# Reordering the first twenty-four products of batch 0, and loading and using the last four 128-row blocks of w_out in two slices

## The chip, the cores and the metric

The kernel runs on one core of one Trainium2 chip. Its time is the device time of one execution in microseconds (us). Most executions of one kernel agree within about 0.1% here. The span of a profile is the time from its first to its last instruction; it is 1.7 to 1.9 us shorter than the device time of the same run.

Names of engines: PE is TensorE's matmul unit, PEld its weight load, DVE is VectorE, ACT is ScalarE, POOL is GpSimd, SP is SyncE. PSUM and SBUF are two memories of the core: in this kernel the matmuls write their sums to PSUM and read what they multiply from SBUF. "L465" means line 465 of the kernel file. Lines below the change have other numbers in other files (the last products are L912 in before and L917 in after).

## The reference, cut to what matters

```python
def _attn_ref(q, k, v, g_norm):            # q, k, v: 8 batches, 8 heads, 576 rows, 64
    kv = np.einsum('bhsd,bhse->bhde', k, v)
    out = np.einsum('bhsd,bhde->bhse', q, kv)
    rms = np.sqrt(np.mean(out * out, axis=-1, keepdims=True) + 1e-06)
    return (out / rms * g_norm).astype(np.float32)

def _moe_ref(x, w_in, w_out):              # x: 4608 x 512, w_in: 512 x 2048, w_out: 2048 x 512
    h = x @ w_in
    g = np.where(h > 0.0, h, np.exp(np.minimum(h, 0.0)) - 1.0)
    return (g @ w_out).astype(np.float32)
```

(The factor alpha of the reference, 1.0, is left out.) The attention output of all heads is the x of the second part. The kernel takes 512 of the 576 rows of one batch as a group, and the 64 left over of every batch as a ninth; batch 0 is special, because everything is still being loaded when it starts.

## The kernel before

Two matrix products per group take nearly all of PE's time. The first, x times w_in, is made as 16 column blocks f of 128, each the sum of 4 chunks c of 128 rows, so 64 matmuls of 128x512. After each pair of blocks, ACT and DVE apply the ELU (`elu`), which frees the pair's PSUM. The second, g times w_out, adds 16 terms f for each of four row groups j.

In batch 0 the first six blocks are made by a special piece of code, because chunk c of x exists only when its normalisation is done:

```python
pair = ps_head.tile([P, 2, G], FP32, name="h_ps", tag="kv")
products = {0: pair[:, 0, :], 1: pair[:, 1, :], 2: bank(6), 3: bank(7), 4: bank(0)}
first((0, 1, 2, 3), (0,))        # blocks, chunks: one matmul for each combination, chunk by chunk
mean_first(3); log_first(3); exp_first(3); scale_first(3)    # makes chunk 3 of x, on PE, ACT, DVE
products[5] = bank(1)
first((0, 1, 2, 3), (1, 2))
first((4, 5), (0, 1, 2))
first((0, 1, 2, 3, 4, 5), (3,))
...
for i, parts in enumerate([[(0, 2, pair)]] + single):
    elu(0, i, parts, i == 1)()
head.close()                      # PSUM of the start is given back ...
ps_at = ...; ps_m1 = ...; ps_m2 = ...    # ... and divided anew into the pools of the main loop
for i in range(3, 8):             # blocks 6 to 15, in pairs; i = 3 is the fourth pair
    mm1(0, i, relu=i in (3, 5, 7), home={5: "m2", 6: "at"}.get(i, "m1"))()
```

`elu` of a pair is an Exp on ACT, then two operations on DVE; the second one reads the products from PSUM again (for the pairs with `relu`, the second and some others, ACT reads them a second time instead). Cut to the case of the first pair:

```python
nc.scalar.activation(e[:, lo:hi, :], ps, AF.Exp)
...
nc.vector.tensor_scalar(out=e[...], in0=e[...], scalar1=1.0, scalar2=1.0, op0=ALU.min, op1=ALU.subtract)
nc.vector.tensor_tensor(out=gT[T][...], in0=e[...], in1=h, op=ALU.max)
```

The loads of w_out go through one queue that POOL issues. "Rows 12 to 14" is short for the blocks 12 and 13 of its 16 blocks of 128 rows, one for each term f. The second product of batch 0 uses them in slices (`hold` puts off the copy of a finished result), with pieces of batch 1's attention put between them:

```python
load_w_out(10, 12)
load_w_out(12, FC)               # FC is 16
fetch_packed_q(2)                # q, then k and v, of batch 2
...
at["mulu1"]()                    # DVE writes the second half of xs of batch 1
unpack_q(2, Q)
ahead["qd"]()
for j in range(J):               # J is 4
    mm2(0, j, 12, FC, hold=j > 1)
    if j == 2:
        at["xu1"](scores[:, 1, :])
mm2_out(0, 2)
mm2_out(0, 3)
...
for i in range(8):               # first product of batch 1
    mm1(1, i, ...)
```

`xu1`, the "turn" in what follows, transposes the second half of batch 1's xs with 8 PE transposes into PSUM, and one DVE operation (L422) copies the result, scaled, to SBUF as chunks 2 and 3 of batch 1's x. The first block of batch 1 needs chunk 2 in its third matmul.

## Time and profile before

| | before |
|---|---|
| median (range of the first 3 runs) | 285.01 us (284.91 to 285.03) |
| span of the profiled run | 283.3 us |
| PE busy | 277.0 us, 98% |
| distance from start to start of two 512-column matmuls | 216 ns |
| only PE wait on the wait list after the first 8 us | 0.3 us, on DVE |

The first and second parts of the page of before say what bounds the kernel:

```profile
PE 277.0 (98%) x2146; PEld 129.2 (46%) x2146; DVE 159.6 (56%) x231; ACT 153.4 (54%) x221; POOL 54.3 (19%) x95
...
PEclk9999999999999999999999999999999999999999
```

PE is busy nearly always, and its granted clock is 90% of full or more in each of the 40 slices (0.998 in the mean). With matmuls at this pace and no less work, only fewer or shorter pauses of PE can make the kernel faster. Pauses must be read with care, for the Trainium skill (Perfetto Trace Analysis, "Tensor Engine Instruction (MATMUL, LD_WEIGHTS)") says that the end of a matmul in a trace is estimated and not observed. This trace agrees: after the head, nearly every 512-column matmul of the full array is shown as 379 ns long (376 to 390), but the next one starts 216 ns after it. So a pause is measured here from start to start, less 216 ns.

The wait list of before (PE only; columns: who waited for whom, total us, times, longest):

```profile
PE bank L596 <- DVE zeros L573: 1.2, 1, 1.2
PE bank L614 <- DVE q_two L150: 0.7, 1, 0.7
PE h_ps L465 <- DVE gT L496: 0.3, 1, 0.3
```

The first two are at the very start. The third is the fifth pair of blocks in batch 0. The chain of waits of before, in order of time, shows what it is made of (start us, duration us, what):

```profile
18.90 0.45 PE h_ps L674 x2
19.35 0.02 issue
19.37 1.03 ACT elu_e L477
20.41 0.02 issue
20.43 0.44 DVE elu_e L488
20.87 0.03 issue
20.89 0.02 DVEq L496
20.91 0.04 issue
20.96 1.23 DVE gT L496
22.19 0.04 issue
22.23 3.61 PE h_ps L465 x16
```

The pair of blocks 0 and 1 is finished by PE at 19.35, read by ACT, and freed by DVE at 22.19. Then the fifth pair, whose PSUM it is, may start. The timeline of PE in before shows the same place (start, duration, engine, line, operation, shapes, count, idle before):

```profile
20.04 1.89 PE L465 MATMUL h_ps<-xT,w_in_sb 128*128 128x512 bf16 x8
22.23 3.61 PE L465 MATMUL h_ps<-xT,w_in_sb 128*128 128x512 bf16 x16 [0.31 <-DVE gT L496]
```

In start times, the last matmul of the fourth pair starts at 21.547 and the first of the fifth at 22.235: 688 ns, so 472 ns lost. The profile's 0.31 us is smaller because the modelled 379 ns still counts as busy.

The turn in the timeline of PE in before:

```profile
45.62 0.61 PE L413 MATMUL se_ps<-ident,xs 128*128 128x128 bf16 x8
46.06 1.03 PE L512 MATMUL o_ps<-w_out_sb,gT 128*128 128x512 bf16 x4
46.92 1.89 PE L465 MATMUL at<-xT,w_in_sb 128*128 128x512 bf16 x8
```

and in the timeline of DVE in before, with the copy that uses them:

```profile
46.34 0.75 DVE L422 TENSOR_SCALAR xT<-se_ps,g_col 128x1024 bf16<-128x1024 bf16 x1 [1.24 <-PE se_ps L413]
```

The copy ends at 47.09. The third matmul of batch 1's first product, the first to read what it wrote, starts at 47.357. It did not have to wait: four matmuls of w_out and two of its own block stood between, and the eight of its line are evenly spaced.

### The profile page before, as it was taken

The page shows a single profiled execution, that of the slowest core. Times are in us where ns is not written, and L with a number is a line of the kernel's source. Part 1 is how long each engine was busy: PE and PEld are TensorE (multiplying, and loading weights), DVE is VectorE, ACT ScalarE, POOL GpSimd, SP SyncE. Part 2 cuts the span into 40 slices and gives each one's busy share as a digit, 9 for nine tenths or more (in the row PEclk, how much of TensorE's full clock was granted, in tenths as well). Part 3 has the DMA queues.
Part 4 walks back from the last instruction along what each step waited for, and adds up shares of the span by engine and source line. Part 5 has one row for each costly group of instructions (what it writes and reads, how often), then busy time and mean ns, then how long its engine had stood idle before and what let it go on. Part 6 is the DMA issues. An engine that isn't in the chain of part 4 may idle for free.

```text
span 283.3 us, 5185 instructions
## 1 busy us (share of the span) xinstructions
PE 277.0 (98%) x2146; PEld 129.2 (46%) x2146; DVE 159.6 (56%) x231; ACT 153.4 (54%) x221; POOL 54.3 (19%) x95
## 2 busy tenths in 40 slices
PE   7999999999999999999999999999999999999994
PEld 2444454445444444444444444444444444444443
DVE  2349543877478646933694468545864586444400
ACT  2769646666486438534773378236923692333311
POOL 7834402161421231005110421012000000000000
PEclk9999999999999999999999999999999999999999
DMA  7999999697994595358934794455233123010122
GB/s 192 203 204 202 206 203 185 218 146 135 194 178 66 152 178 137 74 148 108 212 74 135 104 208 79 117 120 152 50 96 78 78 50 98 0 76 0 74 74 76
DMA packets 56507, 35.99 MB, mean 127 GB/s; under 512 B 32804, under 2 KB 54052, under 8 KB 56484
## 3 DMA queue, kind: packets, MB, share of 16 engines
q0 software_dynamic: 20736, 17.30, 40.1%
q1 hardware_dynamic: 35348, 17.83, 23.8%
q10 hardware_dynamic: 400, 0.52, 0.5%
q8 instruction: 17, 0.28, 0.4%
q14 instruction: 6, 0.05, 0.1%
HBM read 36.70 MB, written 9.44 MB: 163 GB/s over the span
## 4 chain that ended last, share of the span: by engine, by line
PE 95%; DMA 2%; DVE 1%; ACT 0%; issue 0%; SPq 0%; DVEq 0%
PE h_ps L465 41%; PE o_ps L512 39%; PE o_ps L912 5%; DMA st_q<-in_q_dram 2%; PE at L174 2%; PE at L465 1%; PE at L201 1%; PE bank L674 1%; PE h_ps L674 1%; PE bank L596 1%; PE bank L644 1%; PE se_ps L201 1%; DVE gT L496 0%; PE kv_ps L174 0%; ACT elu_e L477 0%; PE at L185 0%
## 5 line engine op out<-in xcount | busy, mean ns | idle before, releaser
L465 PE MATMUL h_ps<-xT,w_in_sb 128*128 128x512 bf16 x536 | 125.8, 379 | 0.3 <-DVE gT L496 0.3
L512 PE MATMUL o_ps<-w_out_sb,gT 128*128 128x512 bf16 x512 | 120.5, 379 | 0.0
L477 ACT ACTIVATE elu_e<-h_ps 128x1024 bf16<-128x1024 f32 (+1 forms) x71 | 70.0, 995 | 81.8 <-PE h_ps L465 79.6
L465 PEld LDWEIGHTS <-w_in_sb 128*128 128x128 bf16 x552 | 52.5, 98 | 64.1 <-DVE xT L333 1.7
L512 PEld LDWEIGHTS <-gT 128*128 128x128 bf16 x512 | 49.4, 98 | 58.4
L488 DVE TENSOR_SCALAR elu_e<-elu_e 128x1024 bf16<-128x1024 bf16 (+1 forms) x75 | 32.2, 429 | 72.5 <-ACT elu_e L477 72.5
L496 DVE TENSOR_TENSOR gT<-elu_e,h_ps 128x1024 bf16<-128x1024 bf16 (+1 forms) x52 | 61.4, 1180 | 5.8 <-DVE elu_e L488 0.5
L525 ACT COPY o_sb<-o_ps 128x512 f32<-128x512 f32 x32 | 18.5, 586 | 15.8 <-PE o_ps L512 15.8
L218 DVE TENSOR_REDUCE ss<-sq 128x16 f32<-128x1024 bf16 x16 | 19.4, 1219 | 10.9 <-ACT sq L213 10.2
L150 POOL COPY q_bf<-q_pk 128x512 bf16<-128x512 bf16 x24 | 14.6, 640 | 22.8 <-DMA q_pk<-in_q_dram 22.8
L483 ACT ACTIVATE elu_h<-h_ps 128x1024 bf16<-128x1024 f32 (+1 forms) x19 | 18.5, 988 | 0.0
L496 DVE TENSOR_TENSOR gT<-elu_e,elu_h 128x1024 bf16<-128x1024 bf16 x19 | 13.2, 692 | 2.8 <-ACT elu_h L483 1.5
L912 PE MATMUL o_ps<-w_out_sb,gT 128*128 128x512 bf16 (+1 forms) x80 | 14.1, 337 | 0.0
L125 POOL COPY gate<-qT 1x1 bf16<-1x1 bf16 x6 | 1.1, 182 | 62.9 <-DMA qT<-q_bf 62.9
L104 POOL DMA_DIRECT2D q_pk<-in_q_dram x14 | 10.5, 755 | 4.0 <-DMA w_out_sb<-in_moe_w_out_dram 1.8
L229 DVE TENSOR_TENSOR xs<-at,ss 128x512 bf16<-128x512 f32 x16 | 10.2, 682 | 1.2 <-ACT ss L225 1.2
L912 PEld LDWEIGHTS <-gT 128*128 128x128 bf16 x80 | 7.7, 98 | 6.4 <-DVE gT L496 0.4
L213 ACT ACTIVATE sq<-at 128x1024 bf16<-128x1024 f32 x9 | 9.4, 1043 | 1.6 <-PE at L201 1.0
L118 POOL DMA_DIRECT2D k_pk<-in_k_dram x12 | 8.3, 692 | 4.6 <-DMA w_in_sb<-in_moe_w_in_dram 2.9
L118 POOL DMA_DIRECT2D v_pk<-in_v_dram x12 | 8.4, 700 | 3.7 <-DMA w_out_sb<-in_moe_w_out_dram 2.1
L596 PE MATMUL bank<-zeros 128*128 128x512 bf16 x20 | 7.4, 495 | 1.2 <-DVE zeros L573 1.2
L920 ACT COPY o_last<-o_ps 128x512 f32<-128x512 f32 (+1 forms) x5 | 2.5, 501 | 10.8 <-PE o_ps L912 10.8
(79 smaller groups left out, 138.2 us busy)
## 6 DMA issues: line engine op xcount, KB each, us to landing
out_dram<-o_sb SPq DMA_DIRECT2D x16, 512.0 KB, 3.0
q_pk<-in_q_dram POOLq DMA_DIRECT2D x14, 256.0 KB, 4.8
k_pk<-in_k_dram POOLq DMA_DIRECT2D x6, 576.0 KB, 8.2
v_pk<-in_v_dram POOLq DMA_DIRECT2D x6, 576.0 KB, 11.5
w_out_sb<-in_moe_w_out_dram POOLq DMA_DIRECT2D x3, 512.0 KB, 14.8
st_q<-in_q_dram SPq DMA_DIRECT2D x2, 512.0 KB, 4.9
w_in_sb<-in_moe_w_in_dram POOLq DMA_DIRECT2D x2, 512.0 KB, 8.9
st_q<-in_q_dram SPq DMA_DIRECT2D x16, 64.0 KB, 2.7
```

The lines of the kernel that those rows point to most:

```text
L104: nc.gpsimd.dma_start(out=t[:, 4 * s : 4 * s + 4].rearrange("p h j d -> p h (j d)"), in_=in_[:, s])
L118: nc.gpsimd.dma_start(out=raw[name, b].rearrange("p h j d -> p h (j d)")[:, hs], in_=in_[:, hs])
L150: eng.tensor_copy(out=out_, in_=in_)
L218: nc.vector.reduce_sum(out=ss, in_=sq.rearrange("p c (h e) -> p (c h) e", h=H), axis=AX.X)
L465: nc.tensor.matmul(h_ps[a][:, cs], lhsT=w_in_sb[:, c, f * P : f * P + P], rhs=x(c, cs), start=(c == 0), stop=(c == KC - 1),)
L477: nc.scalar.activation(e[:, lo:hi, :], ps, AF.Exp)
L483: nc.scalar.activation(h[:, lo:hi, :], ps, AF.Relu)
L488: nc.vector.tensor_scalar(out=e[:, lo:hi, :], in0=e[:, lo:hi, :], scalar1=1.0, scalar2=1.0, op0=ALU.min, op1=ALU.subtract,)
L496: nc.vector.tensor_tensor(out=gT[T][:, 2 * i + lo : 2 * i + hi, :], in0=e[:, lo:hi, :], in1=h, op=ALU.add if relu else ALU.max,)
L512: nc.tensor.matmul(o_ps[T, j], lhsT=gT[T][:, f, j * P : j * P + P], rhs=w_out_sb[:, f, :], start=(f == 0), stop=(f == FC - 1),)
L525: nc.scalar.copy(o_sb[T][:, j % 2, :], o_ps.pop((T, j)))
L912: nc.tensor.matmul(ps, lhsT=gT[B][:, f, j * P : j * P + P], rhs=w_out_sb[:, f, cols], start=(f == 0), stop=(f == FC - 1),)
```

## The change

The intent, as the code suggests: finish blocks 0 to 3 as soon as chunk 3 of x exists, so that ACT and DVE can start on them while PE makes block 5; and because PE is then earlier, let it start on rows 12 and 13 of w_out before rows 14 and 15 have landed.

```diff
     first((0, 1, 2, 3), (1, 2))
-    first((4, 5), (0, 1, 2))
-    first((0, 1, 2, 3, 4, 5), (3,))
+    first((4,), (0, 1, 2))
+    first((0, 1, 2, 3), (3,))
+    first((5,), (0, 1, 2))
+    first((4, 5), (3,))
...
     load_w_out(10, 12)
-    load_w_out(12, FC)
+    load_w_out(12, 14)
+    load_w_out(14, FC)
...
     for j in range(J):
-        mm2(0, j, 12, FC, hold=j > 1)
+        mm2(0, j, 12, 14)
+    for j in range(J):
+        mm2(0, j, 14, FC, hold=j > 1)
         if j == 2:
             at["xu1"](scores[:, 1, :])
```

No matmul and no byte is added or removed. One DMA becomes two.

## The prediction

> **What bounds the kernel.** TensorE. The page gives PE 277.0 of a 283.3 us span (98%), full granted clock in all 40 slices, and a chain of waits that is 95% PE. In the ordered trace a 512-column matmul follows the last every 216 ns, the isolated gap of the Trainium skill (TensorE: Matmul & The Clock Gate, "Back-to-back issue gap"; its sustained 131 ns is not seen here). Matmul ends are estimates, so I reckon start to start. A change can only win where that exceeds 216 ns. The change touches one such place: from 21.547 to 22.235 us, 688 ns, so 472 ns lost (the wait view counts 0.3 us of it, PE h_ps <- DVE gT). The fifth pair of products needs the PSUM pair of the first two: last c=3 matmul of that pair starts 18.957 -> ACT Exp 19.37 to 20.39 -> DVE 0.43 + 1.22 us, done 22.18 -> PE 22.235.
>
> **Part 1, the reorder.** No matmul is added. x0 chunk 3 is written by DVE until 17.965, usable about 18.02 (chunk 2 showed 53 ns from DVE end to PE start); in the new order f=0, c=3 issues at 18.094, so no new stall. The pair is complete three matmuls (647 ns) earlier; Exp starts about 18.73, DVE releases the pair about 21.54, before PE asks at 21.763. The whole 0.47 us goes. The loads have slack enough for PE to stay early: v_pk of batch 1 landed 38.13, used 39.08; w_out rows 10-12 landed 39.38, used 40.80.
>
> **Part 2, split load and slices.** Rows 12-16 landed at 41.94; PE will ask at 42.55 instead of 43.03, so even the unsplit load would just make it. The split costs one more issue on POOL (0.74 us, idle engine), no bytes; rows 12-14 land near 40.7. It buys slack, not time. Later loads on that queue move by under 1 us, off the path.
>
> **What it gives back.** The slices move the transposes of batch 1's second half (xu1). Before, four w_out matmuls plus two of mm1 (c=0, 1) stood between them and the first use of their result; after, only two plus two. Before: first transpose 45.615, DVE copy 46.335 to 47.086, semaphore 47.10, first use 47.357 without wait. From first transpose to usable is 1.52 us; the new order covers 8 transposes (0.447) + 4 x 0.216 = 1.31 us. A new stall of 0.21 us at c=2 of batch 1's first product. The same pattern at 71.540 to 71.902 (362 ns, waiting on DVE xT) shows that such a stall is real.
>
> **Sum.** -0.47 + 0.21 = -0.26 us; after 50 us everything is only shifted: **284.75 us**, range 284.45 to 285.05. Chances: faster by over 2%: 0; within 2%: 0.99; slower: 0.01.
>
> **What would show it.** Right: 216 ns instead of 688 at the fifth pair; first Exp about 18.73; PE never waiting on w_out; about 430 ns start to start before the third matmul of batch 1's first product, released by DVE xT; span about 283.05. Wrong: a stall at f=0, c=3 on x0; a stall on a load between 35 and 45 us; no gap at xu1 (then about 284.55); a growing wait at 70 to 92 us, where DVE waits of 0.15 and 0.19 us exist.
>
> **What would make it wrong.** The load queue pushed back by the extra issue; the copies of the first two outputs, now later on ACT, delaying a PSUM release; run-to-run spread (0.12 us), half the effect.

## The result, and the profile after

| | before | after |
|---|---|---|
| median of 6 runs | 284.98 us (284.83 to 285.06) | 284.75 us (284.56 to 285.67) |
| span of the profiled run | 283.3 us | 283.0 us |
| PE lost before the fifth pair of batch 0 | 472 ns | 0 |
| PE lost at the third matmul of batch 1 | 0 | 214 ns |

The ratio of after to before is 0.9997 (95% interval 0.9984 to 1.001). Ratios and intervals follow the means of the runs more than the medians that are quoted. One of the six runs of after took 285.67 us and pulls that mean up. By the clock alone the change is therefore within noise; the traces have to say whether a gain is there.

The wait list of after, PE only, has lost its third line:

```profile
PE bank L596 <- DVE zeros L573: 1.2, 1, 1.2
PE bank L614 <- DVE q_two L150: 0.5, 1, 0.5
```

The chain of waits of after runs through PE where it had gone through ACT and DVE, and goes through DVE at a place where it had not:

```profile
17.12 1.08 PE bank L674 x5
18.20 0.43 PE h_ps L674 x2
18.64 1.51 PE bank L674 x7
20.15 5.18 PE h_ps L465 x24
...
45.69 0.46 PE se_ps L413 x8
46.15 0.03 issue
46.18 0.02 DVEq L422
46.20 0.05 issue
46.24 0.76 DVE xT L422
47.01 0.04 issue
47.05 1.46 PE at L465 x6
```

The pair is finished ("18.20 0.43 ... h_ps L674 x2", ending 18.64) 0.7 us earlier than in before, and PE goes from the fourth into the fifth pair without a step through another engine. In the timeline of PE in after the two pairs are now one line, and the turn looks like this:

```profile
19.98 4.26 PE L465 MATMUL h_ps<-xT,w_in_sb 128*128 128x512 bf16 x19
...
45.52 0.61 PE L413 MATMUL se_ps<-ident,xs 128*128 128x128 bf16 x8
45.97 0.59 PE L512 MATMUL o_ps<-w_out_sb,gT 128*128 128x512 bf16 x2
46.40 2.10 PE L465 MATMUL at<-xT,w_in_sb 128*128 128x512 bf16 x8
```

Eight matmuls now take 2.10 us, where they took 1.89 in before. That 0.21 us is the whole trace of the new wait on this view. No idle time is printed: the matmul before it starts at 46.619 and is modelled to end at 46.998, so only 51 ns appear idle before the late one starts at 47.049. Start to start it is 430 ns. The wait list leaves it out altogether, but the chain of waits finds it.

The loads, as issue and landing of each part of w_out on the queue (us, read from the trace):

```
rows      before: issued  landed  first used     after: issued  landed  first used
10 to 12          27.20   39.38   40.80                 27.44   39.31   40.28
12 to 14          28.53   41.94   43.03                 28.77   40.59   42.50
14 to 16          with the line above                   31.35   41.92   44.23
```

PE never waited for w_out in either kernel. The four loads behind w_out (q, k and v of batch 2) were issued 1.5 to 2.1 us later in after (the first at 32.78 instead of 31.12, the last at 37.30 instead of 35.22) but landed within 0.1 us of their times in before (43.25 against 43.30, 50.29 against 50.28).

One more reading is needed for the comparisons below. The start of the kernel, up to about 14.5 us, hangs on the first loads and varies between executions: in the eleven traces, the first product of x and w_in starts between 14.24 and 14.62 us. To leave that out, I measure PE's stretch: from the start of the matmul of block 3, chunk 2 (the last one before the orders part) to the start of the kernel's last matmul. It is 261.950 us in before and 261.683 in after: 0.267 us less, against the 0.26 us predicted. It is read from one execution of each kernel; three experiments below that should agree (part1_only, load_split_only, turns_earlier) do so within 0.01 us.

### The profile page after: what moved, and what is told of

It reads as the page before. It is cut to its first block, busy times and chain, and to the rows that moved or that the text cites. A ratio compares the mean times of both kernels' runs of the same rounds, so it can differ in the third digit from the quotient of the medians.

```text
span 283.0 us, 5186 instructions
## 1 busy us (share of the span) xinstructions
PE 277.2 (98%) x2146; PEld 129.4 (46%) x2146; DVE 159.7 (56%) x231; ACT 153.5 (54%) x221; POOL 54.4 (19%) x96
## 4 chain that ended last, share of the span: by engine, by line
PE 95%; DMA 2%; DVE 1%; issue 0%; SPq 0%; ACT 0%; DVEq 0%
PE h_ps L465 42%; PE o_ps L512 39%; PE o_ps L917 5%; DMA st_q<-in_q_dram 2%; PE at L174 2%; PE bank L674 1%; PE at L465 1%; PE at L201 1%; PE h_ps L674 1%; PE bank L596 1%; PE bank L644 1%; PE se_ps L201 1%; PE kv_ps L174 0%; PE at L185 0%; PE se_ps L413 0%; DVE xT L422 0%
```

## The experiments

The theory: PE's time is its matmuls plus the pauses where it waits. The reorder removes one of 0.47 us; the use of w_out in slices creates one of 0.21 us because the turn then has too few matmuls behind it; the split load does neither. The rivals: the split load is needed for the reorder's gain; the extra DMA is what costs 0.2 us; the order of the products counts only by "earlier is better". The first four runs were on one chip, the next four on another, the last on a third, each with runs of before beside it. All gave correct results.

| run | median us (runs) | before beside it (9 or 7 runs) | PE's stretch less that of before | lost before the fifth pair | lost at the turn |
|---|---|---|---|---|---|
| after | 284.75 (6) | 284.98 (6 runs) | -0.27 us | 0 | 214 ns |
| part1_only | 284.50 (5) | 284.92 | -0.48 | 0 | 0 |
| part2_only | 285.21 (5) | 284.92 | +0.20 | 471 ns | 214 ns |
| load_split_only | 284.60 (5) | 284.92 | -0.47 | 0 | 0 |
| turns_earlier | 284.53 (5) | 284.92 | -0.48 | 0 | 0 |
| one_earlier | 284.68 (4) | 285.01 | -0.23 | 256 ns | 0 |
| too_early | 285.13 (4) | 285.01 | +0.09 | 0, but 576 ns at chunk 3 | 0 |
| both_turns | 284.44 (5) | 285.01 | -0.64 | 0 | 0 |
| late_split | 285.53 (4) | 285.01 | +0.57 | 0, but 822 ns on w_out | 215 ns |
| late_whole | 286.60 (4) | 284.94 | +1.52 | 0, but 2005 ns on w_out | 0 |

A caution for who reads such traces: in eight of the nine experiments 31 of the 2146 matmul records are missing (their pages say PE x2115 beside PEld x2146). A missing record looks like a distance of 431 or 432 ns, nearly the same as the real wait at the turn. Where I say that a matmul waited at the turn, all eight matmuls of that block are in the trace and DVE's L422 is what released it.

### part1_only: the reorder without the split

```diff
-    first((4, 5), (0, 1, 2))
-    first((0, 1, 2, 3, 4, 5), (3,))
+    first((4,), (0, 1, 2))
+    first((0, 1, 2, 3), (3,))
+    first((5,), (0, 1, 2))
+    first((4, 5), (3,))
```

> The reorder alone; load and slices as before. Theory: the 688 ns distance in front of the fifth pair becomes 216 ns, rows 12-16 land at 41.9 before PE asks at 42.5, no wait at the third matmul of batch 1's first product: 0.47 us under before, 284.5 us, 0.2 us under the full change. Rival (the split load is what lets PE stay early): a PE wait on w_out near 42.5 us that gives 0.2 us or more back, so 284.75 us or slower.

Measured: 284.50 us, ratio 0.9985 (0.9972 to 0.9997), and PE's stretch 0.48 us shorter than in before. Rows 12 to 16, in one load, landed at 41.59, and PE first used them at 42.25. In the timeline of PE in part1_only the two pairs run on without idle time, and the block after the turn takes 1.89 us:

```profile
19.73 3.62 PE L465 MATMUL h_ps<-xT,w_in_sb 128*128 128x512 bf16 x16
...
46.15 1.89 PE L465 MATMUL at<-xT,w_in_sb 128*128 128x512 bf16 x8
```

So the first part alone is better than the whole change by 0.21 us of PE's stretch, and the rival that the split is needed falls.

### part2_only: the split without the reorder

```diff
-    load_w_out(12, FC)
+    load_w_out(12, 14)
+    load_w_out(14, FC)
...
-        mm2(0, j, 12, FC, hold=j > 1)
+        mm2(0, j, 12, 14)
+    for j in range(J):
+        mm2(0, j, 14, FC, hold=j > 1)
```

> Split load and slices alone; products in the old order. Theory: the fifth pair still waits (688 ns), and a wait of 0.21 us (430 ns start to start) appears at the third matmul of batch 1's first product: 0.21 us over before, 285.2 us. Rival (the split helps by itself): 285.0 or less.

Measured: 285.21 us, ratio 1.0008 (0.9995 to 1.002), PE's stretch 0.20 us longer. Both pauses are there, in the timeline of PE in part2_only:

```profile
22.05 1.24 PE L465 MATMUL h_ps<-xT,w_in_sb 128*128 128x512 bf16 x5 [0.31 <-DVE gT L496]
...
46.31 0.59 PE L512 MATMUL o_ps<-w_out_sb,gT 128*128 128x512 bf16 x2
46.74 2.10 PE L465 MATMUL at<-xT,w_in_sb 128*128 128x512 bf16 x8
```

The two parts add up: -0.48 + 0.20 = -0.28 us, against -0.27 us for both.

### load_split_only: two loads, one slice

```diff
(the reorder, as in part1_only)
-    load_w_out(12, FC)
+    load_w_out(12, 14)
+    load_w_out(14, FC)
```

> The reorder and the split load, but rows 12-16 used in one slice as before. Theory: the new wait comes from the place of the transposes, so it is gone: 216 ns there, 284.5 us as with the reorder alone. Rival (the extra DMA issue causes the loss): the 0.2 us stays, 284.75 us.

Measured: 284.60 us, PE's stretch within 0.01 us of part1_only's, 215 or 216 ns everywhere in the block after the turn, which the timeline of PE in load_split_only shows as

```profile
46.35 1.89 PE L465 MATMUL at<-xT,w_in_sb 128*128 128x512 bf16 x8
```

The extra DMA costs PE nothing; the loss belongs to the use in slices.

### turns_earlier: the whole change, with the turn two matmuls earlier

```diff
         mm2(0, j, 14, FC, hold=j > 1)
-        if j == 2:
+        if j == 1:
             at["xu1"](scores[:, 1, :])
```

> The full change, with the transposes of batch 1's second half one row group earlier (after j=1 instead of j=2 in the last slice, two matmuls earlier). Theory: cover in front of the first use goes from 1.31 to 1.74 us against the 1.52 us needed, the 430 ns distance becomes 216 ns: 284.5 us. xs is ready 0.4 us before. Rival (extra issue): 430 ns stays somewhere, 284.75 us.

Measured: 284.53 us, PE's stretch again that of part1_only (0.003 us apart), and four matmuls of w_out stand behind the turn again. In the timeline of PE in turns_earlier:

```profile
46.40 1.89 PE L465 MATMUL at<-xT,w_in_sb 128*128 128x512 bf16 x8
```

The first transpose to the third matmul of the block is 1.741 us without a wait; in after it is 1.524 us with one. So what the turn needs is 1.524 us, and it is only its place that was wrong.

### one_earlier and too_early: how much earlier is right

one_earlier lets block 5 have two of its three matmuls first, so that the pair is finished one matmul earlier than in before and not three:

```diff
-    first((4, 5), (0, 1, 2))
-    first((0, 1, 2, 3, 4, 5), (3,))
+    first((4,), (0, 1, 2))
+    first((5,), (0, 1))
+    first((0, 1, 2, 3), (3,))
+    first((5,), (2,))
+    first((4, 5), (3,))
```

> A dose: products in an order where the first four finish one matmul (216 ns) earlier than before, instead of three; load and slices as before. Theory: the distance in front of the fifth pair falls by just that, from 688 to about 472 ns; 284.75 us. Rival (any reorder that takes product 5 out of the way frees the whole gap, or the gap depends on ACT and DVE alone): 216 or 688 ns.

Measured: 284.68 us. The distance before the fifth pair is 472 ns, so 256 ns are lost: 216 less than in before, for one matmul of 216 ns. The chain of waits of one_earlier still goes through DVE:

```profile
20.65 1.23 DVE gT L496
21.88 0.04 issue
21.93 1.24 PE h_ps L465 x5
```

too_early puts nothing between chunks 2 and 3:

```diff
-    first((4, 5), (0, 1, 2))
-    first((0, 1, 2, 3, 4, 5), (3,))
+    first((0, 1, 2, 3), (3,))
+    first((4, 5), (0, 1, 2, 3))
```

> The first four products finished with no other product between chunks 2 and 3, then 4 and 5; load and slices as before. Theory: f=0, c=3 would issue at 17.45 but chunk 3 of x0 is usable at 18.02, so PE loses 0.57 us there (788 ns start to start); the fifth pair's gap is gone (216 ns); net +0.10 us, about 285.1 us. Rival (earlier is always better): under 284.6 us.

Measured: 285.13 us, PE's stretch 0.09 us longer than in before. The gap before the fifth pair is gone, and a longer one has opened, where chunk 3 of x is not there yet. In the timeline of PE in too_early:

```profile
17.89 0.59 PE L674 MATMUL h_ps<-xT,w_in_sb 128*128 128x512 bf16 x2 [0.41 <-DVE xT L665]
```

That is 792 ns after the matmul before it, so 576 ns lost. Earlier is not always better: there is a window between the arrival of chunk 3 and the latest time at which the pair may be finished, and the order of the change lies inside it. In after, block 0's chunk 3 matmul starts at 18.040, straight after its forerunner, while the DVE operation that makes chunk 3 ends at 17.90 (17.15 + 0.75). The order lies near the early edge of the window: where PE does wait for a chunk, it starts 53 ns after DVE's end (16.532 to 16.585 for chunk 2 in before), so after had about 84 ns to spare. In load_split_only, with the same order, that matmul did start 53 ns after DVE's end, 230 ns after its forerunner: 14 ns lost.

### both_turns: the same rule at a second place

The lesson of turns_earlier was tried where batch 2's x is made. There, too, before waits after a turn (71.540 to 71.902, 362 ns):

```diff
(turns_earlier, and)
-    mm2_quarter(1, 2, 0)
+    mm2(1, 2, 0, 2)
     at["x1"](...)
-    mm2_quarter(1, 2, 1)
+    mm2(1, 2, 2, 8)
```

> As turns_earlier, and the same rule applied at the second place: batch 2's second-half transposes two matmuls earlier inside the w_out products of batch 1. Theory: the 364 ns distance at 71.6 us becomes 216 ns; 0.15 us more, 284.35 us, faster than both kernels. Rival (the wait there is set by something else, such as xs): 364 ns stays or moves to the transposes.

Measured: 284.44 us, ratio 0.9979 (0.9966 to 0.9991), the lowest median of all, with a stretch 0.64 us shorter than in before (turns_earlier: 0.48). The timeline of PE in turns_earlier, which has that turn in its old place:

```profile
69.92 0.61 PE L305 MATMUL xt_ps<-ident,xs 128*128 128x128 bf16 x8
70.37 1.03 PE L512 MATMUL o_ps<-w_out_sb,gT 128*128 128x512 bf16 x4
71.38 0.61 PE L465 MATMUL h_ps<-xT,w_in_sb 128*128 128x512 bf16 x2
```

and in both_turns:

```profile
69.63 0.61 PE L305 MATMUL xt_ps<-ident,xs 128*128 128x128 bf16 x8
70.08 1.46 PE L512 MATMUL o_ps<-w_out_sb,gT 128*128 128x512 bf16 x6
71.38 0.59 PE L465 MATMUL h_ps<-xT,w_in_sb 128*128 128x512 bf16 x2
```

Above, 70.37 + 4 x 0.216 = 71.23, but the next block starts at 71.38, so it waited. Below, 70.08 + 6 x 0.216 = 71.38: no wait. It beats before by the clock; it was not timed beside after, and that it beats after is read from the stretch (261.308 us against 261.683).

### late_split and late_whole: what the split would be good for

If PE does not wait for w_out, the split cannot show its worth. So the load was made late on purpose, behind batch 2's q, once in two parts and once whole:

```diff
late_split (from after)             late_whole (from part1_only)
-    load_w_out(12, 14)             -    load_w_out(12, FC)
-    load_w_out(14, FC)                  fetch_packed_q(2)
     fetch_packed_q(2)              +    load_w_out(12, FC)
+    load_w_out(12, 14)
+    load_w_out(14, FC)
```

> The full change, with the loads of rows 12-14 and 14-16 issued behind batch 2's two q loads. Theory: 12-14 land near 43.2 against PE asking at 42.5, so a wait of 0.7 to 0.8 us; 14-16 land near 44.6, before their use at about 45.0; about 285.5 us.

> The reorder alone, with the unsplit load of rows 12-16 issued behind batch 2's two q loads. Theory: all four rows land near 44.6 against PE asking at 42.5, a wait of about 2.1 us on w_out; about 286.6 us, 1.1 us over the split load in the same late place. Rival (the split has no worth even when the load is late): the same time as late_split.

Measured: 285.53 us and 286.60 us. In late_split rows 12 to 14 landed at 43.42 and 14 to 16 at 44.66; in late_whole all four landed at 44.48. The timeline of PE in late_split:

```profile
43.46 2.75 PE L512 MATMUL o_ps<-w_out_sb,gT 128*128 128x512 bf16 x12 [0.66 <-DMA w_out_sb<-in_moe_w_out_dram]
```

and in late_whole:

```profile
44.52 1.67 PE L512 MATMUL o_ps<-w_out_sb,gT 128*128 128x512 bf16 x7 [1.84 <-DMA w_out_sb<-in_moe_w_out_dram]
```

Start to start, 0.82 us are lost in the first and 2.01 us in the second. With a late load the split is worth 1.18 us of waiting for 0.21 us at the turn. In the place where the change has it, no trace shows it used: the unsplit load was in time there too (part1_only).

## Why the prediction was right

The median came out as predicted (284.75 us). That it agrees to the last digit is luck, since the six runs lie between 284.56 and 285.67 us. The stated range, 284.45 to 285.05 us, holds the median of before as well, so a change without any effect would have fallen into it too. What counts is that each term of the sum was found where it had been placed.

- **What bounds the kernel, and where a gain can be.** Right. The later part of the kernel only moved: from the turn's third matmul on, after is earlier than before by 0.31 us (47.049 against 47.357, and 97.762 against 98.074 at batch 3's attention). Of that, 0.05 us is the start of the kernel, which varies.
- **Part 1.** Right. The distance before the fifth pair fell from 688 to 216 ns; the first Exp starts at 18.67 (predicted 18.73, and this execution was 0.05 us early). part1_only shows the 0.47 us alone, one_earlier shows that it comes matmul for matmul, and too_early shows the other bound of the window.
- **Part 2.** Right that it buys slack and no time: load_split_only and part1_only are equal. Rows 12 to 14 landed at 40.59 (predicted 40.7). That the unsplit load would still be in time is shown by part1_only, 0.66 us to spare. That later loads on the queue "move by under 1 us" holds for their landing (under 0.1 us) and not for their issue (1.5 to 2.1 us); PE felt nothing of either.
- **What it gives back.** Right in place, cause and size: 430 ns start to start, released by DVE's copy, in after, in part2_only and (431 ns) in late_split; gone when the turn moves.
- **A later wait that grows.** It did not: the distances at 71 and 90 us were 362 and 409 ns in before and are 364 and 408 ns in after.
- **Not foreseen.** That the wait list would not print the new wait at all. And a small pause at chunk 2 of x in batch 0, 91 ns in before and 103 ns in after, differs from execution to execution (nothing of it in part2_only and load_split_only, 125 ns in turns_earlier). Where it is there, PE starts 52 to 55 ns after the end of the DVE operation that makes chunk 2. Why that operation comes earlier in two executions stays open: the first product started at 14.448 us in part2_only and at 14.452 in turns_earlier, so the time at which the kernel's start ends does not decide it. It lies before the stretch that is compared here.

That the timed ratio alone could not tell after from before is no contradiction: the expected 0.26 us is 0.09%, and its interval is 0.26% wide. For part1_only, turns_earlier and both_turns the interval lies below 1, for late_split and late_whole above; for the others it holds 1 or touches it, and there the traces alone decide.

## What to carry to other kernels

On an engine that is as busy as PE here, this reorder was worth just the pauses that it removed less those that it made. So write down for each place how much work stands between a producer on another engine and its first use, and how long that producer needs. When a loop is cut into slices, everything that had been placed by its index ("after j = 2") gets another distance to its use and must be placed anew. Change one thing at a time: here the first half of the change alone beat the whole, and the second half paid only when the load was made late.

## What the Trainium skill lacked or had wrong

- **TensorE: Matmul & The Clock Gate, "Back-to-back issue gap".** It gives 131 ns per matmul as the sustained roofline for 512 columns in a stream of weight load and matmul pairs, and calls 216 ns the isolated gap that over-counts. In all eleven traces, such streams run at 216 ns from start to start (nearly always 215 to 217, at a mean granted clock of 0.997 or more); 131 ns was seen nowhere. The point is against this section alone: other sections of the same page give about 216 ns for back-to-back matmuls.
- **Perfetto Trace Analysis, "Tensor Engine Instruction (MATMUL, LD_WEIGHTS)".** It says that ends are estimated, and the traces agree (379 ns shown, 216 ns apart). It doesn't say what follows: a pause of up to 379 - 216 = 163 ns leaves no idle time at all on the PE row, and every longer one looks 163 ns shorter. The 472 ns pause was shown as 0.31 us, and the 214 ns pause was left with 51 ns and was missing from the wait list.
- **Perfetto Trace Analysis, "Identifying Dependency Chains".** It says that an instruction with waits on several engines may have an EventSemaphore instruction put before it, but gives no cost. Here the DVE copy with one wait (L314) started 24 ns after PE's semaphore (71.069 to 71.093 in before), and the one with two waits (L422) 96 ns after it (46.239 to 46.335), with the extra wait instruction between. That is part of why the turn needs 1.52 us.
- **DMA: Bandwidth & Descriptors.** No section that I found tells what splitting one POOL-issued load costs when POOL has to wait for earlier loads before it issues the next. Here it cost one more issue of 0.7 us on a POOL with time to spare, and nothing in landing: rows 12 to 16 landed at 41.94 whole, and at 40.59 and 41.92 in halves.
- **Perfetto Trace Analysis** does not warn that matmul records can be missing from a trace: 31 of 2146 in eight of the eleven traces. One that is missing among 512-column matmuls leaves a distance of about 431 ns, which looks like a wait of 215 ns.
